# A two-layer linear-attention and MLP kernel: another order of work between the key sums and the dense layer

## The chip, the cores and the metric

The kernel runs on one core of a Trainium2 chip. Five engines work side by side there, each through its own queue of instructions in order: TensorE (PE) multiplies, VectorE (DVE), ScalarE (ACT) and GpSimd (POOL) work on rows of numbers, SyncE (SP) issues transfers. They wait for one another through semaphores. The metric is the device time of one execution in microseconds (us), as the median of several runs.

## The reference

Two identical layers, each with an attention and an MLP part, on 2048 tokens of width 576, with 32 heads of 18 and a hidden width of 4608. The weights are the same in both layers.

```python
x = x + attention(layernorm(x))
x = x + mlp(layernorm(x))          # and both lines once more

def attention(x):
    q, k, v = split_heads(x @ wqkv)                    # 32 heads of 18
    phi_q = concat(softmax(q @ w_phi), softmax(-q @ w_phi))
    phi_k = concat(softmax(k @ w_phi), softmax(-k @ w_phi))
    kv = phi_k^T @ v;  z = sum of phi_k over all tokens
    o = (phi_q @ kv) / (phi_q . z + 1e-6)
    return o @ wo

def mlp(x):
    return relu(x @ w1 + b1)**2 @ w2 + b2
```

The numbers are 32-bit floats. A product of two of them is computed as three: each operand is split into a high part in the format fp32r and a low part (the rest), and high x high, high x low and low x high are added up.

## The kernel before

**Blocks and tiles.** The tokens are worked on in four blocks of 512, each of four tiles of 128. The sums `kv` and `z` run over all tokens, so no query can be finished before the last key is in. The function `barrier` (names t0 in layer 0, t1 in layer 1) holds the passage from the one to the other, with the next stretch of work woven in so that PE has something to do. This passage is what the change edits, once in each layer.

**The passage, in order.** The queries of its block are projected, the last keys go into the sums, and the softmax parts of the queries are formed, `Q0e` to `Q3e`, one for each tile. `sums_operands` makes the operands of the attention product from the sums: `zb` (the sums of keys, spread over all partitions), and the state `kv` masked by head and split, high part `kbh` on ACT, low part `kbl` on DVE. `last_group` does this for the last group of heads, from a product with a mask, `kq`. `g_phi` then scales each tile's features by the denominator: `phi_products` forms `fm`, features times `zb`, one half on DVE and the other on POOL; `phi_sums` adds them up per head on DVE (`fu`); `phi_factors` makes the factor; `phi_scale` multiplies the features by it, half 0 on DVE and half 1 on POOL. Meanwhile PE projects the queries of another block.

`g_out` then works in two parts of two tiles each. In each part `turn` transposes the scaled features on PE (`opt`), ACT writes the high parts and DVE the low ones (`of`); `times` multiplies them with `kbh` and `kbl` (`opn`), and ACT and DVE split the result into `ooh` and `ool`, the last piece being `oolt`. Between the parts stand the scalings of tiles 2 and 3 and, for the two tiles that are done, `x_after`: 30 products with the output weights `oo0h`, `oo0l`, `oo1h`, `oo1l` (`opo`), added to the residual `ox`. After the second part the same follows for tiles 2 and 3, together with the norm of the block, `g_norm`: DVE takes statistics (`begin`) and scales the tile (`scale`), PE transposes it (`onp`; the last 64 columns of two tiles together in `transpose_rest`), ACT and DVE split it (`onh`, `onl`). Each tile then gets the bias `b2` added on POOL and is stored for the end of the MLP (`keep`).

`g_mlp` follows. `first` loads a piece of both MLP weights and splits it (high parts on ACT, low parts on POOL for the first two pieces of this block), `hidden` forms the products with the normed block (`m_3ph` in layer 0, `m_1ph` in layer 1), for the first two pieces in two halves of columns (tiles 0 and 1, then 2 and 3), `square` applies the activation, and `second` adds into the accumulators (`m_3acc`).

In layer 0 the output weights are split in this passage, high parts on ACT and low parts on POOL, and stored to memory; layer 1 loads the stored parts.

**What sets the order.** Work is given out by Python generators, and a scheduler keeps each engine's instructions in an order of its own. `tc.issue_after(ins)` puts what is issued under it behind `ins` in the queue of the engine that both use, without a wait. `held` runs a generator with each step behind named instructions, `chained` puts each step behind the step before it on DVE, ACT and POOL, and `lagged` runs a producer some steps ahead of its consumer.

Of the kernel before, what the change touches and what calls it, by code (L numbers as in the profile page):

```python
# [13 lines left out]
P = 128  # L14
# [7 lines left out]
def layers_kernel(  # L22
# [109 lines left out]
    def chained(gen, strict=False):  # L132
        ends, engines = {}, (nc.vector.engine, nc.scalar.engine, nc.gpsimd.engine)
        while True:
            traced = nc.cur_bb.bb.instructions
            mark = len(traced)
            if strict:
                ends[nc.tensor.engine] = traced_on(nc.tensor)
            with ExitStack() as behind:
                for ins in ends.values():  # L140
                    behind.enter_context(tc.issue_after(ins))
# [253 lines left out]
    def g_norm(x_of, dst, name, then=None, fine=False):  # L395
# [60 lines left out]

        if not fine:
            yield from lagged(NT, scale, turn_all)
            return
# [144 lines left out]
    def sums_operands(layer):  # L604
# [22 lines left out]
        def keep(own, parts):  # L627
            hi, lo = parts
            nc.scalar.activation(hi, own, AF.Copy)
            nc.vector.tensor_sub(lo, own, hi.bitcast(F32))  # L630


        for s in range(2):
# [12 lines left out]
        def last_group():  # L646
            w = gw[last]
            own = sb.tile([P, TB], F32, tag="hr", name=f"kq{layer}", bufs=2)
            own = own[:, : 2 * w].rearrange("p (s q f) -> p s q f", s=2, q=NQ)
            nc.vector.tensor_mul(own, kv[:, :, HG].unsqueeze(2).to_broadcast([P, 2, NQ, DH]),  # L650
                                 quarter.unsqueeze(1).unsqueeze(3).to_broadcast([P, 2, NQ, DH]))
            pt = wtile(f"kt{layer}2")
            p3 = pt[:w, : 2 * w].rearrange("p (s n) -> p s n", s=2)
            with tc.issue_after(dense["projected"].ins):
                for s in range(2):
                    nc.tensor.matmul(p3[:, s], own[:, s].rearrange("p q f -> p (q f)"),
# [77 lines left out]
    def phi_scale(e, r):  # L734
        for s in range(2):
            e3 = e[:, s].rearrange("p (h d) -> p h d", d=DH)
            (nc.gpsimd if s else nc.vector).tensor_mul(
# [30 lines left out]
    def g_out(layer, b, ph, dst, name, parts=1, pause=None, behind=None, norm=None, mid=None, costs=(None, None)):  # L768
# [50 lines left out]
        def x_after(t):  # L819
# [14 lines left out]
            return x  # L834
# [21 lines left out]
        def x_next(t):  # L856
            return xs_of[t] if t < len(xs_of) else x_after(t)

        norms = (norm or g_norm)(x_next, dst, f"{name}n", keep)
        for t in range(len(xs_of)):  # L860
            for _ in held(norms, ("part",)):
                break
        if xs_of:
# [768 lines left out]
```

## Time and profile before

| | |
|---|---|
| median of 3 runs | 2520.44 us (2519.8 to 2522.17) |
| profiled execution | 2522.92 us |
| its span (first to last instruction) | 2521.2 us |
| busy share of the span | PE 98%, PE's weight loads 86%, DVE 62%, ACT 50%, POOL 38% |
| mean granted PE clock | 0.994 |
| transfers | 348.52 MB, mean 138 GB/s |

All times in the text come from the profiled execution unless it says otherwise. An engine's busy time is the time with an instruction at work; a row that ends in a bracket gives the idle time of the engine just before the instruction and what ended it. The granted clock is the speed that PE was given, 1.00 being full.

### The profile page before, as it was taken

What the parts mean: (1) busy time and instruction counts of PE and PEld (TensorE: products, weight loads), DVE (VectorE), ACT (ScalarE), POOL (GpSimd) and SP (SyncE); (2) the same over time, 40 slices, a digit from 0 to 9 for tenths busy, and PEclk for the clock granted to TensorE, in tenths of its full rate; (3) what the DMA queues carried; (4) which work ended last, traced back from release to release, by engine and by line L of the source; (5) the groups of instructions that cost most, each with busy time, mean ns of one, the idle gap of its engine ahead of it and who ended that gap; (6) DMA issues with size and microseconds to landing.
All of it is one profiled execution on the core that took longest, in us unless ns stands there. A gap on an engine that the chain in (4) does not pass through costs nothing.

```text
span 2521.2 us, 41458 instructions
## 1 busy us (share of the span) xinstructions
PE 2477.4 (98%) x15108; PEld 2176.8 (86%) x15108; DVE 1565.9 (62%) x2514; ACT 1267.1 (50%) x2245; POOL 950.9 (38%) x1101
## 2 busy tenths in 40 slices
PE   8998999999999999999999989999999999999999
PEld 8998888888888888888889988888888888888888
DVE  6778848554856655555657778394548666555454
ACT  4344545453546666664333445454445466666642
POOL 3544312212325555552333443132123355565322
PEclk8999999999999999999999999999999999999999
DMA  9222633356434433328754144333573444333363
GB/s 333 75 70 86 203 112 88 101 167 216 130 119 119 149 109 104 117 85 283 252 185 140 44 150 131 100 98 98 163 241 100 129 129 140 118 95 114 112 199 126
DMA packets 249691, 348.52 MB, mean 138 GB/s; under 512 B 30158, under 2 KB 157262, under 8 KB 246926
## 3 DMA queue, kind: packets, MB, share of 16 engines
q1 hardware_dynamic: 248228, 343.18, 43.4%
q8 instruction: 118, 1.93, 0.3%
q10 hardware_dynamic: 1258, 2.70, 0.3%
q14 instruction: 87, 0.71, 0.1%
HBM read 279.46 MB, written 66.32 MB: 137 GB/s over the span
## 4 chain that ended last, share of the span: by engine, by line
PE 88%; DVE 4%; ACT 2%; DMA 2%; POOL 1%; issue 1%; SPq 1%; DVEq 0%; ACTq 0%; POOLq 0%
PE m_ppx L1227 8%; PE m_pacc L1256 6%; PE m_pacacc L1256 5%; PE m_1ph L912 5%; PE m_3ph L912 5%; PE m_2ph L912 5%; PE m_0ph L912 4%; PE m_ppy L1227 4%; PE m_2acc L939 3%; PE m_0acc L939 3%; PE m_1acc L939 3%; PE m_3acc L939 3%; PE m_pacacc L1246 2%; PE m_pach L1256 2%; PE m_pacc L1246 2%; PE m_ppz L1227 2%
## 5 line engine op out<-in xcount | busy, mean ns | idle before, releaser
L1217 POOL TENSOR_TENSOR m_ps<-m_pr,m_ps 128x128 fp32r<-128x128 f32 x144 | 118.8, 826 | 312.8 <-ACT m_ps L1215 251.6
L1216 DVE TENSOR_TENSOR m_ps<-m_pr,m_ps 128x448 fp32r<-128x448 f32 x144 | 96.9, 673 | 179.3 <-ACT m_ps L1215 174.4
L1256 PE MATMUL m_pacc<-m_ps,m_phb 128*128 128x448 f32 x864 | 188.5, 366 | 0.0
L1256 PEld LDWEIGHTS m_pacc<-m_ps,m_phb 128*128 128x128 f32 x864 | 162.1, 188 | 17.9
L1215 ACT ACTIVATE m_ps<-m_pr 128x576 fp32r<-128x576 f32 x144 | 98.1, 681 | 124.4 <-issue 71.6
L1256 PE MATMUL m_pacacc<-m_ps,m_phc 128*128 128x448 f32 x648 | 149.6, 368 | 0.0
L1256 PEld LDWEIGHTS m_pacacc<-m_ps,m_phc 128*128 128x128 f32 x648 | 119.8, 189 | 9.1
L1237 DVE TENSOR_TENSOR m_phb<-m_pz,m_phb 128x512 fp32r<-128x512 f32 x72 | 56.5, 784 | 111.1 <-ACT m_pz L1236 109.6
L939 PE MATMUL m_0acc<-m_0s,m_0hb 128*128 128x448 f32 x432 | 100.2, 366 | 0.0
L939 PE MATMUL m_2acc<-m_2s,m_2hb 128*128 128x448 f32 x432 | 100.1, 366 | 0.0
L912 PE MATMUL m_1ph<-t1onh,m_1h 128*128 128x512 f32 (+1 forms) x380 | 98.5, 385 | 1.5 <-DVE t1onh L443 0.8
L912 PE MATMUL m_3ph<-t0onh,m_3h 128*128 128x512 f32 (+1 forms) x380 | 98.1, 383 | 1.6 <-DVE t0onh L443 0.8
L939 PE MATMUL m_3acc<-m_3s,m_3hb 128*128 128x448 f32 x432 | 99.5, 365 | 0.0
L939 PE MATMUL m_1acc<-m_1s,m_1hb 128*128 128x448 f32 x432 | 99.5, 365 | 0.0
L912 PE MATMUL m_2ph<-a_2nh,m_2h 128*128 128x512 f32 (+1 forms) x380 | 97.9, 384 | 0.0
L912 PE MATMUL m_0ph<-a_0nh,m_0h 128*128 128x512 f32 (+1 forms) x380 | 97.8, 384 | 0.0
L939 PEld LDWEIGHTS m_0acc<-m_0s,m_0hb 128*128 128x128 f32 x432 | 80.9, 188 | 10.6 <-ACT m_0hb L920 0.2
L939 PEld LDWEIGHTS m_2acc<-m_2s,m_2hb 128*128 128x128 f32 x432 | 80.9, 188 | 10.5 <-ACT m_2hb L920 0.2
L939 PEld LDWEIGHTS m_3acc<-m_3s,m_3hb 128*128 128x128 f32 x432 | 81.0, 188 | 10.4
L939 PEld LDWEIGHTS m_1acc<-m_1s,m_1hb 128*128 128x128 f32 x432 | 81.0, 188 | 10.3
L897 POOL TENSOR_TENSOR m_1s<-m_1r,m_1s 128x128 fp32r<-128x128 f32 x36 | 25.3, 702 | 168.6 <-ACT m_1s L892 155.0
L897 POOL TENSOR_TENSOR m_3s<-m_3r,m_3s 128x128 fp32r<-128x128 f32 x36 | 24.7, 687 | 167.9 <-ACT m_3s L892 160.5
(2440 smaller groups left out, 7366.8 us busy)
## 6 DMA issues: line engine op xcount, KB each, us to landing
m_pr<-in_B_w SPq DMA_DIRECT2D x144, 288.0 KB
m_pr<-in_B_w SPq DMA_DIRECT2D x72, 256.0 KB
hd<-m_pu SPq DMA_DIRECT2D x72, 256.0 KB
m_pg<-hd SPq DMA_DIRECT2D x72, 256.0 KB
m_3r<-in_B_w SPq DMA_DIRECT2D x36, 288.0 KB
m_2r<-in_B_w SPq DMA_DIRECT2D x36, 288.0 KB
m_1r<-in_B_w SPq DMA_DIRECT2D x36, 288.0 KB
m_0r<-in_B_w SPq DMA_DIRECT2D x36, 288.0 KB
```

The costliest lines, as they stand in the source:

```text
L897: nc.gpsimd.tensor_sub(s2[:, D + R : 2 * D], r2[:, R:], s2[:, R:D].bitcast(F32))
L912: dense["hidden"] = nc.tensor.matmul(ph[:, cols], a, m, start=(k == 0), stop=(k == len(ops) - 1))
L939: nc.tensor.matmul(acc[t][:, :R], a[:, rows], m, start=(f == 0 and k == 0), stop=(f == NF - 1 and k == 2))
L1215: nc.scalar.activation(s2[:, :D], r2, AF.Copy)
L1216: nc.vector.tensor_sub(s2[:, D : D + R], r2[:, :R], s2[:, :R].bitcast(F32))
L1217: nc.gpsimd.tensor_sub(s2[:, D + R : 2 * D], r2[:, R:], s2[:, R:D].bitcast(F32))
L1227: nc.tensor.matmul(ps, a, m, start=start and i == 0, stop=i == len(ms) - 1, skip_group_check=True)
L1237: nc.vector.tensor_sub(hl, r, hh.bitcast(F32))
L1246: nc.tensor.matmul(accs[b][KC], a, m, start=(g == 0 and k == 0), stop=(g == NF - 1 and k == 2))
L1256: nc.tensor.matmul(accs[b][t][:, :R], a[:, rows], m, start=(g == 0 and k == 0), stop=(g == NF - 1 and k == 2))
```

## The change

Six edits, all between the complete key sums and the first MLP products of the block.

1. In layer 0 the split of the output weights is queued later: the high parts behind the last high part of the state (`kbh`) on ACT, the low parts behind the scaling of tile 1 on POOL. Before, both stood behind an earlier eviction.
2. The mask product `kq` moves ahead in `sums_operands` and takes another buffer.
3. The products and sums of tile 2 (`fm`, `fu`) are no longer issued ahead of the first part of `g_out`; they follow it.
4. The norm statistics of tiles 0 and 1 are taken ahead of the second part's transposes, behind DVE's scaling of tile 3.
5. After the second part, one hand-written list, `tail`, replaces the interleaving of residual products and norm: the scaling of tiles 0 and 1, all residual products of tiles 2 and 3, and only then the norm transposes. `chained` gets a mode, `every`, that orders PE's steps as well. The norm of tile 3 (`last`) goes between the hidden products of the first two weight pieces. The additions of `b2` and the stores that follow them come last.
6. The low parts of the first two pieces of MLP weights are queued behind the scaling of tile 3 on POOL.

```diff
@@ chained
+    def chained(gen, strict=False, every=False):
+        ends, engines = {}, [nc.vector.engine, nc.scalar.engine, nc.gpsimd.engine]
+        if every:
+            engines.append(nc.tensor.engine)
...
+            own = {}
             for ins in traced[mark:]:
                 if ins.engine in engines:
-                    ends[ins.engine] = ins
+                    own.setdefault(ins.engine, []).append(ins)
+            for engine, step in own.items():
+                ends[engine] = step if every else step[-1:]
@@ g_norm
+        if fine is None:
+            yield begin, scale, (transpose, split_main), (transpose_rest, split_rest)
+            return
@@ sums_operands
+        kq = sb.tile([P, KC * P], F32, tag="xn", name=f"kq{layer}")
...
+        nc.vector.tensor_mul(kq, ...)
         for s in range(2):
             pt = wtile(f"kt{layer}{s}")
...
@@ phi_scale
-            (nc.gpsimd if s else nc.vector).tensor_mul(
+            dense[f"scaled{s}"] = (nc.gpsimd if s else nc.vector).tensor_mul(
@@ g_out
         def pieces():
-            with tc.issue_after(behind.ins) if behind else nullcontext():
+            with ExitStack() as order:
+                for ins in behind or ():
+                    order.enter_context(tc.issue_after(ins.ins))
                 return wpair("o", name, low=nc.gpsimd if parts > 1 else None)
...
                 xs_of += [x_after(t) for t in range((part - 1) * NT // parts, part * NT // parts)]
+                by_part = next(g_norm(xs_of.__getitem__, dst, f"{name}n", None, None))
+                with tc.issue_after(dense["scaled0"].ins):
+                    owns = [by_part[0](t) for t in range(len(xs_of))]
...
+        def tail():
+            scaled(0)
+            yield
+            scaled(1)
+            yield
+            xs_of.append(x_after(2))
+            yield
+            owns.append(begin(2))
+            yield
+            other = g_after(3)
+            next(other)
+            yield
+            scaled(2)
+            yield
+            xs_of.append(next(other))
+            yield
+            owns.append(begin(3))
+            yield
+            pts = [main[0](t, xns[t]) for t in range(2)]
+            yield
+            for t in range(2):
+                main[1](t, pts[t])
+                yield
+            turned_rest(0)
+            yield
+            scaled(3)
+            yield
+            turned(2)
+            keep(3, xs_of[3])
+            yield
+            for t in range(3):
+                keep(t, xs_of[t])
+
+        with tc.issue_after(dense["part"].ins):
+            drain(chained(tail(), every=True))
+
+        def last():
+            turned(3)
+            yield
+            turned_rest(1)
+            yield
@@ g_mlp
-            (nc.gpsimd if early else nc.vector).tensor_sub(l1, r1, h1.bitcast(F32))
+            with tc.issue_after(dense["scaled1"].ins) if early else nullcontext():
+                (nc.gpsimd if early else nc.vector).tensor_sub(l1, r1, h1.bitcast(F32))
...
-            hidden(f, halves[0])
-        if rest:
-            with tc.issue_after(dense["hidden"].ins):
-                drain(rest)
+            with tc.issue_after(traced_on(nc.tensor)) if rest else nullcontext():
+                hidden(f, halves[0])
+                if rest:
+                    with tc.issue_after(dense["hidden"].ins):
+                        next(rest)
@@ barrier
         drain(queries)
         last_group()
-        next(phi)
         dst = {}
-        drain(g_out(layer, b, ph, dst, f"{n}o", 2, phi, dense["evicted"]))
+        drain(g_out(layer, b, ph, dst, f"{n}o", 2, phi, (kbh, scaled)))
```

Line numbers shift by 6 to 11 in the functions around `g_out`, and by 64 in the products of `g_mlp`. Below, rows of each engine's order show three places.

POOL in layer 0, from its first work behind the softmax parts of the queries on; `oo0r` and `oo1r` are the loaded output weights, `l` their low parts. Before:

```order
L336 TENSOR_TENSOR t0oo0l<-t0oo0r,t0oo0h 126x1152
L336 TENSOR_TENSOR t0oo0l<-t0oo0r,t0oo0h 72x288
L336 TENSOR_TENSOR t0oo1l<-t0oo1r,t0oo1h 126x1152
L719 TENSOR_TENSOR t0fm_2836<-t0fQ0e,zb_2802 128x576
L336 TENSOR_TENSOR t0oo1l<-t0oo1r,t0oo1h 72x288
L719 TENSOR_TENSOR t0fm_2913<-t0fQ1e,zb_2802 128x576
L737 TENSOR_TENSOR t0fQ0e<-t0fQ0e,t0fQ0r 128x576
L719 TENSOR_TENSOR t0fm_2981<-t0fQ2e,zb_2802 128x576
L737 TENSOR_TENSOR t0fQ1e<-t0fQ1e,t0fQ1r 128x576
```

The same place after:

```order
L728 TENSOR_TENSOR t0fm_2838<-t0fQ0e,zb_2802 128x576
L728 TENSOR_TENSOR t0fm_2915<-t0fQ1e,zb_2802 128x576
L746 TENSOR_TENSOR t0fQ0e<-t0fQ0e,t0fQ0r 128x576
L746 TENSOR_TENSOR t0fQ1e<-t0fQ1e,t0fQ1r 128x576
L342 TENSOR_TENSOR t0oo0l<-t0oo0r,t0oo0h 126x1152
L342 TENSOR_TENSOR t0oo0l<-t0oo0r,t0oo0h 72x288
L342 TENSOR_TENSOR t0oo1l<-t0oo1r,t0oo1h 126x1152
L342 TENSOR_TENSOR t0oo1l<-t0oo1r,t0oo1h 72x288
L728 TENSOR_TENSOR t0fm_3115<-t0fQ2e,zb_2802 128x576
```

The four low parts moved from ahead of the two tiles' products and scalings to behind them, and ahead of tile 2's product.

DVE in layer 0, from the scaling of tile 0 to the first low part of the transposed features. Before:

```order
L650 TENSOR_TENSOR kq_2973<-kv_862,quarter 128x144
L737 TENSOR_TENSOR t0fQ0e<-t0fQ0e,t0fQ0r 128x576
L731 RECIPROCAL t0fu_2916<-t0fu_2916 128x32
L719 TENSOR_TENSOR t0fm_2980<-t0fQ2e,zb_2802 128x576
L732 TENSOR_TENSOR t0fQ1r<-t0fQ1r,t0fu_2916 128x64
L725 TENSOR_REDUCE t0fu_2984<-t0fm_2980 128x32
L737 TENSOR_TENSOR t0fQ1e<-t0fQ1e,t0fQ1r 128x576
L725 TENSOR_REDUCE t0fu_2984<-t0fm_2981 128x32
L630 TENSOR_TENSOR kbl_2804<-kt_2975,kbh_2803 72x2x72
L796 TENSOR_TENSOR t0of_3016<-t0opt_3017,t0of_3016 126x256
```

After:

```order
L746 TENSOR_TENSOR t0fQ0e<-t0fQ0e,t0fQ0r 128x576
L740 RECIPROCAL t0fu_2918<-t0fu_2918 128x32
L741 TENSOR_TENSOR t0fQ1r<-t0fQ1r,t0fu_2918 128x64
L746 TENSOR_TENSOR t0fQ1e<-t0fQ1e,t0fQ1r 128x576
L639 TENSOR_TENSOR kbl_2804<-kt_2975,kbh_2803 72x2x72
L805 TENSOR_TENSOR t0of_3009<-t0opt_3010,t0of_3009 126x256
```

Tile 2's product, its two sums and the mask product no longer stand between the two scalings and the first split.

PE in layer 0, near the end of the output-weight products. Before, from the middle of the products of tile 2 into those of tile 3:

```order
L830 MATMUL t0opo_3372<-t0oo1h,t0ooh 128x288
L421 MATMUL t0onp_3344<-ident,t0onn_3326 128x128 x4
L830 MATMUL t0opo_3372<-t0oo1l,t0ooh 128x288
L830 MATMUL t0opo_3372<-t0oo1h,t0ool 128x288
L830 MATMUL t0opo_3372<-t0oo1h,t0ooh 128x288
L830 MATMUL t0opo_3372<-t0oo1l,t0ooh 128x288
L830 MATMUL t0opo_3372<-t0oo1h,t0oolt 128x288
L435 MATMUL t0onp_3409<-ident,t0one 128x128
L830 MATMUL t0opo_3416<-t0oo0h,t0ooh 128x288
L830 MATMUL t0opo_3416<-t0oo0l,t0ooh 128x288
L830 MATMUL t0opo_3416<-t0oo0h,t0ool 128x288
L421 MATMUL t0onp_3402<-ident,t0onn_3339 128x128 x4
```

After, from the last products of tile 3 on:

```order
L841 MATMUL t0opo_3406<-t0oo1l,t0ooh 128x288
L841 MATMUL t0opo_3406<-t0oo1h,t0oolt 128x288
L427 MATMUL t0onp_3431<-ident,t0onn_3334 128x128 x4
L427 MATMUL t0onp_3436<-ident,t0onn_3337 128x128 x4
L441 MATMUL t0onp_3447<-ident,t0one 128x128 x2
L427 MATMUL t0onp_3455<-ident,t0onn_3403 128x128 x4
L976 MATMUL m_3ph_3486<-t0onh,m_3h_0_3481 128x256 x5
L976 MATMUL m_3ph_3486<-t0onl,m_3h_0_3481 128x256 x4
L976 MATMUL m_3ph_3486<-t0onh,m_3h_0_3481 128x256 x5
L427 MATMUL t0onp_3501<-ident,t0onn_3452 128x128 x4
L976 MATMUL m_3ph_3519<-t0onh,m_3h_1_3514 128x256 x5
```

The norm's transposes of tiles 0 to 2 (`onp`), which stood among the products with the output weights, now stand behind the last of them, and those of tile 3 behind the first half of the first hidden products.

More of the change, by code (lines that the diff above doesn't have):

```diff
@@ L628, in keep @@
             hi, lo = parts
-            nc.scalar.activation(hi, own, AF.Copy)
+            dense["kbh"] = nc.scalar.activation(hi, own, AF.Copy)
             nc.vector.tensor_sub(lo, own, hi.bitcast(F32))
+        kq = sb.tile([P, KC * P], F32, tag="xn", name=f"kq{layer}")
+        kq = kq[:, : 2 * gw[last]].rearrange("p (s q f) -> p s q f", s=2, q=NQ)
+        nc.vector.tensor_mul(kq, kv[:, :, HG].unsqueeze(2).to_broadcast([P, 2, NQ, DH]),
+                             quarter.unsqueeze(1).unsqueeze(3).to_broadcast([P, 2, NQ, DH]))
         for s in range(2):
@@ L1400, in g_attend @@
             yield from mid[0]
-        yield from g_out(layer, b, ph, dst, name, behind=behind and behind["last"], norm=norm, mid=mid[1],
+        yield from g_out(layer, b, ph, dst, name, behind=behind and (behind["last"],), norm=norm, mid=mid[1],
                          costs=(1.0, None if norm else 3.0))
```

49 lines of the change are left out of this document (24 added, 25 removed).

## The prediction

> **What bounds the kernel now.** I read the page first, then the waits of TensorE (PE), then the chain of waits and the timelines of the two places that the change edits, the barriers t0 (layer 0) and t1 (layer 1). PE is busy for nearly the whole span, so only its idle time, or time at a low clock, can be won. The stages view cuts each barrier at four points: PE's last covered projection, the end of `t0oolt` of the first part, that of the second part, and the first product into the accumulators.
>
> ```profile
> PE 2477.4 (98%) x15108; PEld 2176.8 (86%) x15108; DVE 1565.9 (62%) x2514; ACT 1267.1 (50%) x2245; POOL 950.9 (38%) x1101
> 210.43:218.30 7.87, 1.34 (x7) 0.74 (x5) 7.87 (x15) 1.50 (x4) 4.90 (x4) 0.65 0.00 0
> 218.30:227.88 9.58, 9.58 (x62) 9.58 (x63) 6.75 (x18) 5.31 (x15) 5.07 (x5) 0.76 0.52 155
> 227.88:242.77 14.89, 13.92 (x109) 13.34 (x108) 13.52 (x33) 5.22 (x15) 2.85 (x2) 1.00 0.15 45
> 242.77:264.95 22.18, 18.31 (x134) 16.66 (x133) 13.79 (x33) 5.38 (x11) 8.79 (x12) 1.00 0.61 222
> 1456.50:1466.46 9.96, 7.96 (x69) 7.77 (x68) 8.90 (x22) 6.40 (x19) 6.95 (x6) 1.00 0.27 72
> 1466.46:1481.36 14.90, 13.93 (x109) 13.36 (x108) 13.52 (x34) 5.21 (x15) 2.85 (x2) 1.00 0.30 98
> 1481.36:1504.49 23.13, 19.35 (x134) 18.09 (x133) 13.80 (x34) 5.75 (x11) 8.80 (x12) 0.93 0.62 224
> ```
>
> In a row stand the stretch, its length, the busy time of PE, its weight loads, DVE, ACT and POOL, and the granted clock. Layer 0 needs 54.52 us from the first cut to the last, layer 1 47.99. Nearly all of the difference lies in the first part (17.45 against 9.96), though both compute the same. The chain, POOL's timeline and PE's waits say why:
>
> ```profile
> 200.52 7.78 DVE kbl L630 x2
> 1446.58 2.40 DVE kbl L630 x2
> 197.18 3.95 POOL L336 TENSOR_TENSOR t0oo0l<-t0oo0r,t0oo0h 126x1152 fp32r<-126x1152 f32 x2 [4.27 <-ACT t0oo0h L335]
> 201.10 2.67 POOL L336 TENSOR_TENSOR t0oo1l<-t0oo1r,t0oo1h 126x1152 fp32r<-126x1152 f32 x1
> 205.12 0.80 POOL L336 TENSOR_TENSOR t0oo1l<-t0oo1r,t0oo1h 72x288 fp32r<-72x288 f32 x1
> PE t0opt L793 <- DVE t0fQ1e L737: 3.4, 1, 3.4
> PE t1opt L793 <- DVE t1fQ1e L737: 2.0, 1, 2.0
> ```
>
> The same two DVE subtractions take 7.78 us beside POOL's low parts of the output weights and 2.40 us without them. DVE's chain to the scaled features Q1e is then 5.4 us late, and PE waits for it.
>
> **The change, part by part.** First part. The anchor is ACT's last sum (`zb`).
>
> ```profile
> 197.96 0.29 ACT L625 ACTIVATE zb<-z 128x144 f32<-128x144 f32 x1 [0.37 <-PE z L623]
> 1444.07 0.29 ACT L625 ACTIVATE zb<-z 128x144 f32<-128x144 f32 x1 [1.12 <-PE z L623]
> 1455.20 1.73 DVE L719 TENSOR_TENSOR t1fm<-t1fQ2e,zb 128x576 f32<-128x576 f32 x1
> 1456.99 0.73 DVE L725 TENSOR_REDUCE t1fu<-t1fm 128x32 f32<-128x576 f32 x1
> 1457.65 1.33 DVE L737 TENSOR_TENSOR t1fQ1e<-t1fQ1e,t1fQ1r 128x576 f32<-128x576 f32 x1
> 1457.18 0.73 ACT L891 ACTIVATE m_1h<-m_1r 128x640 fp32r<-128x640 f32 x1
> 1459.40 1.21 ACT L795 ACTIVATE t1of<-t1opt 126x256 fp32r<-126x256 f32 x4 [1.49 <-PE t1opt L793]
> 218.81 1.67 ACT L795 ACTIVATE t0of<-t0opt 126x256 fp32r<-126x256 f32 x4 [4.37 <-PE t0opt L793]
> ```
>
> In layer 1 the new DVE order drops the third tile's product (1455.20 to the next start at 1456.85: 1.65) and one of its sums (0.66, start to start) from before Q1e. Q1e, which ended at 1458.98, ends near 1456.65, about when PE has finished its projections. What is late next is ACT: its weight split starts at 1457.18 and ends near 1457.85, so the first eviction starts there instead of at 1459.40, 1.5 earlier. From there to `oolt` ACT and DVE pace the stage, and it moves as a whole: 9.96 becomes 8.45. The constant mask product `kq` that moves ahead lands in an idle stretch of DVE and costs nothing.
>
> Layer 0, counted from `zb`, has PE's projections end at the same point (12.47 against 12.43) but the first eviction 20.85 after it instead of layer 1's 15.33. With the low parts gone from beside DVE it follows layer 1: 8.45 instead of 17.45, **9.0 saved**. Of that, 7.0 is the eviction's earlier start, the rest the half clock in which PE comes back (0.76 over the stage). The low parts now run behind Q1e, 3.95 + 2.67 + 0.80 = 7.4 us at the most, from about 12.9 to 20.3 after `zb`; PE's first product that reads them comes near 18.0, the second weight half's from 21.2 on. That is cover of 1 to 2 us. They are SBUF work on POOL beside DVE splits that read PSUM, which in layer 1 kept their pace beside POOL's weight lows.
>
> Second part. The third tile's product and two sums, taken out above, now stand behind `oolt` and ahead of Q2e and Q3e.
>
> ```profile
> 1466.52 0.75 DVE L719 TENSOR_TENSOR t1fm<-t1fQ3e,zb 128x576 f32<-128x576 f32 x1
> 1469.17 1.69 POOL L737 TENSOR_TENSOR t1fQ2e<-t1fQ2e,t1fQ2r 128x576 f32<-128x576 f32 x1 [5.02 <-DVE t1fu L729]
> 1469.75 1.16 DVE L730 SCALAR_TENSOR_TENSOR t1fu<-t1fu 128x32 f32<-128x32 f32 x1
> 1472.26 1.64 DVE L737 TENSOR_TENSOR t1fQ3e<-t1fQ3e,t1fQ3r 128x576 f32<-128x576 f32 x1
> 1474.74 1.96 DVE L796 TENSOR_TENSOR t1of<-t1opt,t1of 126x256 fp32r<-126x256 f32 x5 [0.47 <-ACT t1of L795]
> 1481.29 1.17 DVE L389 BATCH_NORM_STATS2 t1ons<-t1ox 128x6 f32<-128x288 f32 x3
> ```
>
> That adds 0.67 + 2 x 0.66 = 2.0 to the chain to Q3e. It ended 7.45 after `oolt` and now ends 9.4 after it. PE's products of the first part cover about 6.3 of this, so PE's wait of 0.93 grows to some 2.5. Behind Q3e DVE then has the four statistics (1.17 for three, so 0.39 each) and an aggregate ahead of its first split: 1.95 in place of 0.83, so 1.1 more. The order of the remaining splits is unchanged. So 14.90 becomes **18.0 in each layer, 3.1 lost**. In layer 0 POOL's products of tiles 2 and 3 stand behind the low parts and can hold DVE's up: between 0.3 and 1.0, I take 0.5. Bounds for the loss: 2.0 if PE's head start absorbs the statistics, 4.0 if the splits also wait for ring buffers.
>
> Third stretch. Here PE's stalls go:
>
> ```profile
> 1484.16 0.66 PE L421 MATMUL t1onp<-ident,t1onn 128*128 128x128 f32 x4 [0.61 <-DVE t1onn L410]
> 1487.34 0.66 PE L421 MATMUL t1onp<-ident,t1onn 128*128 128x128 f32 x4 [1.33 <-DVE t1onn L410]
> 1499.37 0.46 PE L912 MATMUL m_1ph<-t1onh,m_1h 128*128 128x256 f32 x1 [0.82 <-DVE t1onh L443]
> 458.87 3.98 PE a_2po L830 x30
> 254.39 3.36 PE m_3ph L912 x26
> ```
>
> PE has the last 45 products of weights left at `oolt`, at 3.98 / 30 = 0.133 each: they end at T = 6.2 after it, with no norm transpose between. Scaling tile 2 now waits for tile 0's transposes, since the two share a buffer (T + 0.65); behind it in DVE's queue stand the last residual add, the statistics of tile 3 (to T + 2.4), two low parts at 0.65 and the tail's low part at 0.45: T + 4.1. PE's first hidden product that needs the tail can start there, after an idle 1.8. Its 10 remaining products (0.12 each), tile 3's transposes, 14 products, the last transposes and 28 products end at T + 11.05, and five products that stand ahead of the accumulators add 1.2: 6.2 + 12.2 = **18.4**, against 22.18 and 23.13. That saves 3.8 and 4.7. Bounds: 2.5 if the low parts slip, 6.0 if the idle 1.8 closes.
>
> Covered moves: the first two hidden weights' lows run on POOL behind Q3e and are done some 5 us before T, when PE needs them after T; the bias adds end near T + 10.5 and can hold DVE's second-layer lows by one add of 1.4, needed at T + 12.3; on SP the residual loads stand behind POOL's low-part stores, leave near 218 and are needed near 224.
>
> The sum: layer 0 8.45 + 18.5 + 18.4 = 45.35 for 54.52, so 9.2 saved; layer 1 8.45 + 18.0 + 18.4 = 44.85 for 47.99, so 3.1 saved. Together 12.3. The profiled execution took 2522.92 us (its span is 2521.2), 2.5 over the median of the runs, 2520.44; taken off the median this gives **2508.1 us**. Its own range, from the bounds, is 2503 to 2514. About 0.2% (5 us) is what a measurement here can tell from no change.
>
> **The rivals.** *The clock.* The same hidden products run at two speeds in the two layers:
>
> ```profile
> 261.13:263.77 2.64, 2.64 (x22) 2.64 (x22) 1.14 (x2) 1.15 (x2) 0.00 (x0) 1.00 1.01 423
> 1499.37:1503.53 4.16, 4.16 (x22) 4.16 (x23) 1.54 (x3) 1.74 (x3) 0.00 (x0) 0.59 1.00 413
> ```
>
> After waits as short as 0.7 and 0.8 the clock fell in layer 1 and not in layer 0, at a price of 1.5. The change makes two longer waits in each barrier (2.5 and 1.8). If each of the four costs 1.5, 6.0 of the 12.3 goes: 2514.1. Against it: the wait of 2.0 in layer 1 left the clock at 1.00 in the stretch behind it. The Trainium skill, "TensorE: Matmul & The Clock Gate", section "What's actually happening", says that the clock halves after at least one idle window of about 3.4 us; by that rule none of the four waits would cost anything, but layer 1's fall behind 0.7 and 0.8 does not agree with it, so the rival keeps its chance.
>
> *The tail gives nothing.* The waits for the norm are not removed but gathered behind the last product, where DVE's queue is one chain. If that chain takes as long as the four stalls did, the 8.5 is gone and 3.8 is left: 2516.6. For it: the chain has ten steps in a row.
>
> *It does not do what it says.* POOL's two feature products now start where the low parts stood, and if they hold `kbl` as long, 5.4 and some 2 of half clock stay: 12.3 - 7.4 = 4.9, so 2515.5. Against it: layer 1 has these products there, and its 2.40.
>
> *Slower: a load in PE's way.* Two products with the state `a_0uh` stand ahead of the accumulators in PE's order.
>
> ```profile
> 255.55 0.37 SPq L489 DMA_DIRECT2D a_0uh<-xth  x1
> 253.00:265.00 12.00, 10.08 (x74) 9.02 (x74) 6.46 (x14) 3.96 (x8) 3.61 (x4) 1.00 0.93 348
> ```
>
> Its load was issued at 255.55 and used at 263.6. Now `a_0q0l` goes ahead of it on SP. These three loads (2.7 MB) take 7.8 us at 348 GB/s; issued from T - 2, they land near T + 6 to T + 8, and PE is there at T + 11. From T + 11 on each microsecond stops PE. The kernel is slower once both layers lose over 6.2, which is a landing at T + 17; at T + 21 it loses 20 and ends at 2528. The margin of 3 us and the measured rate speak against it.
>
> **How the numbers follow.** Forecast 0.70, the clock 0.13, an empty tail 0.06, no relief 0.05, the late load 0.06. Faster by over 0.2% (under 2515.4) are the first two, 0.83; the tail and no relief lie within, 0.11; slower 0.06. The range takes the forecast's bounds and the clock's case and stops at the edge of the others: 2503.5 to 2515.5.
>
> **What would show it.** `kbl` in layer 0 near 2.4; PE's wait for Q1e gone in both layers; the stage to the first `oolt` near 8.5 in both; the second part longer, near 18, with PE's wait for Q3e near 2.5; no PE wait among the products of weights, and one of about 1.8 behind the first hidden products. It is wrong if the second part in layer 0 exceeds 20, if the third stretch stays above 21, or if PE waits for `a_0uh`.

## The result and the profile after

The changed kernel takes 2512.91 us (median of 8 runs, 2508.59 to 2515.48) against 2520.89 (8 runs, 2518.26 to 2523.24): a ratio of 0.9967, 95% interval 0.9956 to 0.9978. It is 8.0 us faster where 12.3 were forecast. The profiled span is 2513.4 us, 7.8 less than before.

The busy times on the page after, and the stages cut at the same four points as before, first layer 0, then layer 1 (stretch, length, busy time of PE, weight loads, DVE, ACT, POOL, then the granted clock):

```profile
PE 2476.7 (99%) x15108; PEld 2172.4 (86%) x15108; DVE 1558.2 (62%) x2514; ACT 1266.0 (50%) x2245; POOL 952.8 (38%) x1101
210.61:218.96 8.35, 8.24 (x69) 7.81 (x68) 5.89 (x17) 6.28 (x19) 8.35 (x7) 1.00 0.39 132
218.96:237.95 18.99, 16.93 (x113) 15.22 (x111) 16.75 (x42) 5.15 (x15) 10.14 (x11) 0.91 0.41 125
237.95:257.40 19.45, 17.16 (x130) 16.14 (x129) 13.14 (x27) 5.20 (x11) 7.15 (x8) 1.00 0.58 216
1448.26:1456.61 8.35, 8.24 (x69) 7.81 (x68) 5.89 (x17) 6.27 (x19) 3.03 (x3) 1.00 0.01 3
1456.61:1476.24 19.63, 18.05 (x113) 16.45 (x111) 16.85 (x43) 5.18 (x15) 8.20 (x10) 0.83 0.31 94
1476.24:1495.23 18.99, 17.31 (x130) 16.20 (x129) 13.44 (x28) 5.20 (x11) 7.52 (x8) 1.00 0.54 210
```

The first part is 8.35 in both layers. The second part is longer than forecast and its clock is below 1.00 in both layers, which it was in neither before. The third stretch is shorter than before, less than forecast. The sums are 46.79 (54.52 before) and 46.97 (47.99): 7.7 and 1.0 saved, 8.75 together, of which the span shows 7.8. Rows of DVE's timeline and PE's waits after (a row of waits names who waited, for whom, and how long in all, how many times, and the longest):

```profile
200.43 2.51 DVE L639 TENSOR_TENSOR kbl<-ko,kbh 126x504 fp32r<-126x504 f32 x2
226.61 1.63 DVE L746 TENSOR_TENSOR t0fQ3e<-t0fQ3e,t0fQ3r 128x576 f32<-128x576 f32 x1
PE m_3ph L976 <- DVE t0onh L449: 2.3, 1, 2.3
PE t0opt L802 <- POOL t0fQ3e L746: 1.1, 1, 1.1
PE m_1ph L976 <- DVE t1onh L449: 1.7, 1, 1.7
PE m_1acc L1003 <- DVE m_1hb L986: 0.4, 1, 0.4
PE m_1acc L1003 <- ACT m_1hb L984: 0.3, 1, 0.3
PE m_1ph L976 <- DVE m_1h L957: 0.3, 1, 0.3
```

`kbl` is back to 2.51 in layer 0, PE's waits for Q1e and for the norm among the products are gone, and three short waits of 1.0 together stand behind layer 1's third stretch, where there were none.

### The profile page after: what moved, and what is told of

It is laid out like the page before. It is cut to its first block, busy times and chain, and to the rows that moved or that the text cites. A ratio compares the mean times of both kernels' runs of the same rounds, so it can differ in the third digit from the quotient of the medians.

```text
span 2513.4 us, 41455 instructions
## 1 busy us (share of the span) xinstructions
PE 2476.7 (99%) x15108; PEld 2172.4 (86%) x15108; DVE 1558.2 (62%) x2514; ACT 1266.0 (50%) x2245; POOL 952.8 (38%) x1101
## 4 chain that ended last, share of the span: by engine, by line
PE 88%; DVE 4%; DMA 2%; ACT 2%; issue 1%; POOL 1%; SPq 1%; ACTq 0%; DVEq 0%; POOLq 0%
PE m_ppx L1292 8%; PE m_pacc L1321 6%; PE m_pacacc L1321 5%; PE m_3ph L976 5%; PE m_2ph L976 4%; PE m_0ph L976 4%; PE m_1ph L976 4%; PE m_ppy L1292 4%; PE m_2acc L1003 3%; PE m_0acc L1003 3%; PE m_3acc L1003 3%; PE m_1acc L1003 3%; PE m_pacacc L1311 2%; PE m_pacc L1311 2%; PE m_ppz L1292 2%; PE m_pach L1321 2%
## 5 line engine op out<-in xcount | busy, mean ns | idle before, releaser
L1003 PEld LDWEIGHTS m_1acc<-m_1s,m_1hb 128*128 128x128 f32 x432 | 80.9, 188 | 11.9 <-DVE m_1hb L986 0.8
L1003 PEld LDWEIGHTS m_3acc<-m_3s,m_3hb 128*128 128x128 f32 x432 | 81.1, 188 | 10.3
L1003 PEld LDWEIGHTS m_0acc<-m_0s,m_0hb 128*128 128x128 f32 x432 | 80.9, 188 | 10.5 <-ACT m_0hb L984 0.2
```

The lines of the kernel that those rows point to most:

```text
L1003: nc.tensor.matmul(acc[t][:, :R], a[:, rows], m, start=(f == 0 and k == 0), stop=(f == NF - 1 and k == 2))
```

## The experiments

Twelve kernels ran, in groups on several chips, each group with its own runs of the kernel before (medians of 2518.78 to 2520.89); the ratios compare across groups better than the medians do. The stages are cut as above, but the third stretch runs to the first product into the accumulators, 0.16 earlier than in the rows above (so 19.29 and 18.83 for the changed kernel).

| kernel | median us | ratio to before (95%) | layer 0: parts 1, 2, 3 | layer 1 |
|---|---|---|---|---|
| before | 2520.89 | | 17.5, 14.9, 22.0 | 10.0, 14.9, 23.0 |
| changed | 2512.91 | 0.9967 (0.9956 to 0.9978) | 8.3, 19.0, 19.3 | 8.3, 19.6, 18.8 |
| edit 1 alone | 2519.26 | 0.9995 (0.9986 to 1.0004) | 9.8, 21.0, 22.7 | 11.8, 14.9, 21.7 |
| edits 1 and 6 | 2513.60 | 0.9972 (0.9963 to 0.9981) | 9.8, 16.9, 22.3 | 11.9, 14.9, 21.7 |
| changed, old tail | 2515.54 | 0.9980 (0.9971 to 0.9989) | 8.3, 18.1, 22.6 | 8.3, 18.3, 21.7 |
| changed, tile 2 ahead | 2512.10 | 0.9971 (0.9962 to 0.9980) | 11.6, 16.1, 20.6 | 10.5, 16.1, 18.9 |
| changed, products twice | 2511.63 | 0.9971 (0.9959 to 0.9982) | 8.3, 17.9, 19.3 | 8.3, 17.9, 20.4 |
| changed, splits earlier | 2512.41 | 0.9971 (0.9961 to 0.9982) | 8.3, 20.0, 18.7 | 8.3, 19.3, 18.3 |
| changed, bias early | 2511.54 | 0.9970 (0.9959 to 0.9982) | 8.3, 19.9, 20.7 | 8.3, 20.3, 20.4 |
| changed, half of tile 2 ahead | 2509.65 | 0.9958 (0.9945 to 0.9970) | 8.3, 17.8, 20.9 | 8.4, 16.6, 18.8 |
| half, splits, bias | 2509.45 | 0.9965 (0.9951 to 0.9978) | 8.3, 17.8, 19.8 | 8.4, 16.7, 20.9 |
| the same with a half projection | 2512.09 | 0.9971 (0.9962 to 0.9980) | 10.1, 17.9, 20.1 | 10.3, 16.7, 21.2 |
| half and splits | 2509.26 | 0.9958 (0.9944 to 0.9971) | 8.3, 18.4, 18.7 | 8.3, 17.9, 18.3 |

**Edit 1 alone** on the kernel before (with `pieces` taking a list of instructions, as in the change):

```diff
-        drain(g_out(layer, b, ph, dst, f"{n}o", 2, phi, dense["evicted"]))
+        drain(g_out(layer, b, ph, dst, f"{n}o", 2, phi, (kbh, scaled)))
```

> The kernel before with edit 1 alone (in layer 0 the output weights' splits queued behind the state on ACT and behind tile 1's scaling on POOL). Theory A, POOL's low parts beside the state's subtraction cost layer 0 its time: the two subtractions fall from 7.78 us to about 2.5, the first part of layer 0 from 17.45 to about 10, as layer 1 has it; layer 1 stays; the total falls by 7 to 7.5 us. Rival B, the relief comes from edit 3, which takes tile 2's product and sums off VectorE's path: the subtractions stay above 6 us, the first part above 15, the total within 2 us of before.

Both were half right. `kbl` fell to 2.51 and the first part to 9.77, as A said, but nothing was won in the total. The stages of layer 0, and what DVE and POOL did at the start of the second part:

```profile
210.78:220.55 9.77, 7.94 (x69) 7.75 (x68) 8.73 (x22) 6.40 (x19) 9.24 (x6) 1.00 0.28 92
220.55:241.52 20.97, 15.90 (x109) 15.40 (x108) 18.13 (x33) 5.48 (x15) 7.36 (x7) 0.84 0.39 123
220.47 3.28 DVE L729 TENSOR_TENSOR t0fu<-t0fu,t0fQ2r 128x64 f32<-128x64 f32 x1
219.74 3.09 POOL L895 TENSOR_TENSOR m_3h<-m_3r,m_3h 128x640 fp32r<-128x640 f32 x2
222.80 0.87 POOL L899 TENSOR_TENSOR m_3s<-m_3r,m_3s 128x128 fp32r<-128x128 f32 x2
```

The output weights' low parts pushed POOL's low parts of the MLP weights back, to where DVE needs its next product: a product of 128x64 (0.21 elsewhere) took 3.28, until POOL was done at 223.67. Tile 3's product on POOL came behind them. The 7.7 won in the first part became 6.1 lost in the second. Layer 0's third stretch lost another 0.7, and layer 1, which edit 1 does not touch, lost 1.8 in its first part, where the clock fell (0.86 of full).

**Edits 1 and 6**, the same with the MLP weights' low parts behind tile 3's scaling too (one of two places in the code is shown):

```diff
-            (nc.gpsimd if early else nc.vector).tensor_sub(l1, r1, h1.bitcast(F32))
+            with tc.issue_after(dense["scaled1"].ins) if early else nullcontext():
+                (nc.gpsimd if early else nc.vector).tensor_sub(l1, r1, h1.bitcast(F32))
```

> The kernel before with edits 1 and 6: the output weights' low parts behind tile 1's scaling on POOL and the first MLP weights' low parts behind tile 3's scaling (edit 1 alone had left them ahead of tile 3's product, and VectorE's first small product of the second part took 3.28 us beside them). Theory A, what edit 1 won in layer 0's first part was given back because POOL's low parts moved beside VectorE's next work: with edit 6 the second part of layer 0 falls from 20.97 to 15 to 17, the first part stays near 9.8, and the total falls by 5 to 7 us against before. Rival B, the second part is long for another reason (the output weights' own low parts are late): it stays above 19, and the total stays within 2 us of before.

```profile
220.65:237.57 16.92, 15.42 (x109) 14.83 (x108) 14.27 (x33) 5.36 (x15) 7.80 (x7) 0.90 0.48 152
220.57 0.75 DVE L729 TENSOR_TENSOR t0fu<-t0fu,t0fQ2r 128x64 f32<-128x64 f32 x1
```

A holds: the small product takes 0.75, the second part 16.92, and the total is 0.9972 of before. The two edits of the weight splits' order alone give most of what the whole change gives: at 0.9972 (0.9963 to 0.9981) against 0.9967 (0.9956 to 0.9978), edits 2 to 5 together add nothing that is clear of the noise. On the kernel before, edit 1 needs edit 6; edit 6 alone and edit 2 alone were not tried.

**The old tail** in the changed kernel (edits 4 and 5 undone, in `g_mlp` too):

```diff
-        with tc.issue_after(dense["part"].ins):
-            drain(chained(tail(), every=True))
...
+        norms = (norm or g_norm)(x_next, dst, f"{name}n", keep)
+        for t in range(len(xs_of)):
+            for _ in held(norms, ("part",)):
+                break
```

> The changed kernel with edits 4 and 5 undone: the norm interleaved with the output products as before, its statistics behind the second part. Theory A, the new tail is worth what the stages say: the third stretch goes back from 19.29 and 18.83 to about 22 and 22 to 23, the second part loses the statistics (1.1), and the total rises by 4 to 5 us over the changed kernel. Rival B, the tail only trades short waits for long ones: the total stays within 2 us of the changed kernel.

```profile
237.95:260.54 22.59, 18.04 (x133) 16.39 (x131) 13.79 (x33) 5.79 (x11) 8.79 (x12) 1.00 0.63 217
1479.85:1501.55 21.70, 17.66 (x132) 16.20 (x131) 13.74 (x33) 5.22 (x10) 8.80 (x12) 1.00 0.60 223
```

The tail shortens the third stretch by 3.3 and 2.9 and lengthens the second by 0.9 and 1.35, a gain of 3.9 in the stages; the medians differ by 2.6 us, and the intervals of the ratios overlap. That lies between the two expectations: A has the mechanism and over-sized it.

**Products twice.** The last half of tile 1's output product is computed twice, its first result thrown away:

```diff
+                for again in range(2 if parts > 1 and t == 1 and half == 1 else 1):
                     for g in range(NG):
```

> The changed kernel with 15 products more in each barrier: the last half of tile 1's output product is computed twice, 15 x 0.133 = 2.0 us of work for TensorE where it now waits 0.36 and 1.11 us ahead of the second part's transposes. Theory A, the fallen clock of the second part costs 1 to 1.6 us in each layer: with the wait filled the clock stays at 1.00, the second part shrinks by 1.0 (layer 0) and 1.6 (layer 1), the total falls by about 2.5 us although work is added. Rival B, the chain of ScalarE and VectorE sets the pace there: the clock stays up and the second part stays within 0.3 us. Rival C, TensorE is the bound: the second part grows by up to 2 us in each layer.

```profile
219.51:237.45 17.94, 16.88 (x128) 15.82 (x126) 16.70 (x43) 5.18 (x15) 10.17 (x11) 1.00 0.43 132
1456.21:1474.15 17.94, 16.88 (x128) 15.81 (x126) 16.70 (x42) 5.18 (x15) 8.23 (x10) 1.00 0.34 103
1474.15:1494.54 20.39, 18.71 (x130) 17.60 (x129) 12.00 (x27) 5.05 (x10) 7.11 (x8) 0.92 0.60 222
```

Fifteen useless products in each barrier make the second part 1.05 and 1.69 shorter, to the same 17.94 in both layers, at a clock of 1.00: A, for the second part to the tenth. So the fallen clock cost 2.7 us in the second parts of the profiled changed kernel. In the total a median lower by 1.3 us is not clear of the noise; layer 1's third stretch lost 1.6 to a fall there.

**The changed kernel once more:**

> The changed kernel once more, to see whether its clock falls at the same places. Theory A, the pattern of short waits ahead of the second part's transposes (0.36, 1.11 and 0.2 us within 3 us, with little work between) lowers the clock each time, and the single wait of 2.3 or 1.7 us in the third stretch only at times: the second part shows 0.83 to 0.91 in both layers again. Rival B, the clock falls at random: the second part shows 1.00 in one layer or both.

```profile
218.04:237.24 19.20, 16.89 (x113) 15.30 (x111) 16.76 (x42) 5.14 (x15) 10.15 (x11) 0.91 0.41 124
1456.92:1476.18 19.26, 16.97 (x113) 15.41 (x111) 16.75 (x42) 5.14 (x15) 8.19 (x10) 0.91 0.32 96
```

Its one run took 2516.09 us. The clock fell in both layers again, and so it did in all five profiles with these waits ahead of the second part (changed, once more, old tail, splits earlier, bias early): 10 barriers of 10.

**Tile 2 ahead** (edit 3 undone):

```diff
         last_group()
+        next(phi)
         dst = {}
```

> The changed kernel with edit 3 undone (tile 2's product and sums ahead of the first part again). Theory A, the second part grew because VectorE's chain to tile 3's scaling is longer, and the wait that this makes also lets the clock fall: the second part goes from 18.99 and 19.63 to about 16 in both layers at a clock of 1.00, the first part from 8.35 to about 9.9; the total falls by 3 to 4 us. Rival B, the early statistics make the wait: the second part stays above 17.5 with a fallen clock, and the total rises by 1 us or stays.

```profile
208.46:220.04 11.58, 9.49 (x69) 9.30 (x68) 8.41 (x21) 6.40 (x19) 9.81 (x6) 0.85 0.36 116
220.04:236.13 16.09, 14.87 (x113) 13.81 (x111) 14.85 (x40) 5.18 (x15) 8.74 (x10) 1.00 0.42 133
1456.74:1472.84 16.10, 14.88 (x113) 13.83 (x111) 14.85 (x40) 5.18 (x15) 8.73 (x10) 1.00 0.27 78
```

The stages are those of A, 16.1 at full clock, but the total is that of the changed kernel: PE's wait for Q1e returns (2.1 and 2.5), and in layer 0 the clock falls there instead, and once more in the third stretch (20.6). Edit 3 as a whole is worth nothing that can be measured; it moves a wait.

**Half of tile 2 ahead.** Only DVE's half of the product and its sum stand ahead, in DVE's idle time:

```diff
+            if t == NT // 2:
...
+                with tc.issue_after(dense["scaled0"].ins):
+                    nc.vector.tensor_mul(ms[0], e[:, 0], zb[:, 0])
+                    nc.vector.tensor_reduce(u[:, 0], ...)
+                yield
+                nc.gpsimd.tensor_mul(ms[1], e[:, 1], zb[:, 1])
+                nc.vector.tensor_reduce(u[:, 1], ...)
...
+        next(phi)
         last_group()
```

> The changed kernel with half of edit 3 undone in VectorE's idle time: VectorE's half of tile 2's product and its sum (0.74 + 0.66 us) stand right behind tile 1's scaling, where VectorE idles 1.73 and 0.59 us. Theory A, the order alone counts: the first part stays at 8.35, the second falls from 18.99 and 19.63 to 16.5 to 17.5 at a clock of 1.00, the total by 3 to 4 us. Rival B, a product of VectorE that begins while POOL runs one instruction behind another waits until POOL's row ends, as the state's subtraction (7.78 us) and the small product (3.28 us) did: in layer 0 the product stands beside POOL's scaling and low parts, takes up to 7 us and adds up to 6 to the first part; in layer 1 it stands beside two products of POOL and adds 1 to 2; the total rises by 2 to 6 us.

```profile
208.54:216.86 8.32, 8.04 (x69) 7.74 (x68) 7.26 (x18) 6.28 (x19) 8.32 (x6) 1.00 0.34 113
216.86:234.66 17.80, 15.18 (x113) 13.86 (x111) 16.03 (x41) 5.18 (x15) 10.09 (x12) 1.00 0.45 143
1452.08:1468.70 16.62, 14.89 (x113) 13.86 (x111) 15.38 (x41) 5.17 (x15) 8.21 (x10) 1.00 0.32 94
207.55 1.73 DVE L758 TENSOR_TENSOR t0fm<-t0fQ2e,zb 128x576 f32<-128x576 f32 x1
206.99 1.68 POOL L746 TENSOR_TENSOR t0fQ1e<-t0fQ1e,t0fQ1r 128x576 f32<-128x576 f32 x1 [0.23 <-DVE t0fQ1r L741]
```

A holds but for layer 0's second part, 17.80 where 17.5 was the bound. DVE's product took 1.73 instead of 0.75, because POOL's scaling ran until 208.67; but it got in ahead of POOL's low parts, and DVE's idle time had room for it. The second part became 1.2 and 3.0 shorter; 1.05 and 1.69 of this are the clock, which stayed up. The median is 3.3 us under the changed kernel's, 2.3 by the ratios, whose intervals overlap; in this profile layer 0's third stretch lost 1.6 to a fall of the clock (20.9).

**Splits earlier.** In `tail`, the transposes and splits of tiles 0 and 1 stand behind `x_after(2)`:

```diff
             xs_of.append(x_after(2))
             yield
+            pts = [main[0](t, xns[t]) for t in range(2)]
+            yield
+            for t in range(2):
+                main[1](t, pts[t])
+                yield
+            turned_rest(0)
+            yield
             owns.append(begin(2))
```

> The changed kernel with another order of the tail: the norm's transposes and splits of tiles 0 and 1 stand behind tile 2's output products instead of behind tile 3's. Theory A, TensorE's wait of 2.29 and 1.68 us ahead of the first hidden products comes from VectorE's queue, in which tile 3's addition, statistics and aggregate and tile 2's scaling stand ahead of the splits: the wait goes, tile 3's own transposes wait up to 1 us instead, the third stretch falls from 19.29 and 18.83 to about 18 and 17.7, the total by 2 to 2.5 us. Rival B, the chain through tile 3's norm sets the end anyway: the wait only moves behind the first hidden products, and the third stretch stays within 0.4 us.

```profile
239.25:257.94 18.69, 17.24 (x128) 15.78 (x126) 13.71 (x27) 5.12 (x10) 7.52 (x8) 1.00 0.46 168
1475.80:1494.10 18.30, 16.73 (x127) 15.75 (x126) 13.75 (x28) 5.11 (x10) 7.54 (x8) 1.00 0.46 163
```

The wait of 2.29 and 1.68 goes; PE waits 1.0 and 1.3 for the scaled tiles 2 and 3 instead. The stretch is 0.6 and 0.5 shorter: between A and B. The total, 2512.41, is not clear of the changed kernel's.

**Bias early.** In `tail`, the additions of `b2` and their stores stand behind the scalings:

```diff
             scaled(1)
             yield
+            keep(0, xs_of[0])
+            keep(1, xs_of[1])
+            yield
             xs_of.append(x_after(2))
...
             turned(2)
-            keep(3, xs_of[3])
             yield
-            for t in range(3):
-                keep(t, xs_of[t])
+            keep(2, xs_of[2])
+            keep(3, xs_of[3])
```

> The changed kernel with the additions of b2 and their stores early: tiles 0 and 1 behind their scaling, tiles 2 and 3 behind tile 3's scaling. Theory A, the bias in last place costs 1 us behind layer 1's third stretch, since the stores stand ahead of the third MLP weight piece on SP's queue, whose load ScalarE waits 3.04 us for: without it the waits of TensorE for m_1hb (0.34 and 0.41 us) and the late load go, and the total falls by about 1 us. Rival B, POOL's additions beside VectorE's scalings and additions of the tail hold them: the third stretch grows by 1 us or more in each layer.

What ACT, POOL and SP show at this place in the changed kernel, behind layer 1's third stretch:

```profile
1487.57 5.96 POOL L870 TENSOR_TENSOR t1ox<-t1ox,b2t 128x576 f32<-128x576 f32 x4 [1.58 <-DVE t1one L417]
1489.02 4.86 SPq L871 DMA_DIRECT2D xm<-t1ox  x4
1497.08 2.10 SPq L238 DMA_DIRECT2D m_1r<-in_B_w  x2
1506.27 0.74 ACT L954 ACTIVATE m_1h<-m_1r 128x640 fp32r<-128x640 f32 x1 [3.04 <-DMA m_1r<-in_B_w]
```

The four stores wait on SP for the last additions, weight loads stand behind them, and ACT waits 3.04 for such a load. With the bias early neither ACT's wait nor any wait of PE is left in the 30 us behind the stretch. That does not show this half of A yet, for in the second profile of the changed kernel the stores stand at the same place (1488.97, 4.86), and there ACT waits 0.50 and PE not at all:

```profile
1503.65 0.74 ACT L954 ACTIVATE m_1h<-m_1r 128x640 fp32r<-128x640 f32 x1 [0.50 <-DMA m_1r<-in_B_w]
```

The total with the bias early (2511.54) is not clear of 2512.91. Its third stretches are longer by 1.4 and 1.6, as B said, but both have a clock of 0.92, and PE's wait in them is the old 2.29 and 1.67: the length is the clock's, and that the additions held the stretch is not shown.

**Half, splits and bias**, the last three diffs together:

> The changed kernel with the three edits of the runs before that helped: VectorE's half of tile 2's product and its sum behind tile 1's scaling, the transposes and splits of tiles 0 and 1 behind tile 2's output products, the additions of b2 early. Theory A, the three act in different stretches and their gains add up: first part 8.3 to 8.4, second part 17.8 (layer 0) and 16.6 (layer 1) at a clock of 1.00, third stretch 18.7 and 18.3, so 44.8 and 43.3 us, 5.3 less than the changed kernel's 46.63 and 46.81 together, and about 1 us behind them: the total falls to 2506 to 2508. Rival B, the gains share a cause (TensorE's clock, which fell in different places in each profile), and the total stays at 2509 or above.

It stays at 2509.45, as B said. With the splits earlier, the early additions do cost something, beside a fall of the clock in layer 1's third stretch (20.9). Rows of DVE and POOL:

```profile
246.65 1.61 DVE L416 TENSOR_SCALAR t0onn<-t0ox,t0onm,t0ond 128x512 f32<-128x512 f32 x1 [0.98 <-POOL t0ond L398]
246.58 1.40 POOL L881 TENSOR_TENSOR t0ox<-t0ox,b2t 128x576 f32<-128x576 f32 x1
```

DVE's scaling of tile 3 (0.55 without the early bias, in the last kernel below) is held until POOL's addition ends at 247.98, and PE waits 1.6 for it.

**A half projection** (14 products of the next block's queries) between the parts, on top of this:

```diff
-        for _ in range(4):
+        for i in range(4):
             next(phi)
-            next(queries)
-            next(queries, None)
+            for _ in range(2 if i < 3 else 0):
+                next(queries)
...
+                with tc.issue_after(traced_on(nc.tensor)):
+                    drain(fill)
```

> The kernel of the run before this with one half projection of the next block's queries (14 products, 1.95 us) moved from ahead of the first part to the place between the parts where TensorE waits 2.1 and 1.3 us for tile 3's scaling. Theory A, useful work fills the wait: the first part begins up to 1 us earlier, after VectorE's scaling of tile 1, the wait for tile 3 goes, and the clock stays up: the total falls by 2 to 3 us against the run before this. Rival B, VectorE and ScalarE set the start of the first part: TensorE waits about 1.5 us there instead, and the total stays within 1 us.

2512.09 us (ratio 0.9971, 0.9962 to 0.9980): no gain, and more likely a loss. In layer 0 the wait for tile 3 fell from 2.1 to 0.8, but PE now waited 0.4, 0.6 and 0.6 for Q1e and `kbl` in the first part and 0.9 in the second, as B said.

**Half and splits**, those two diffs without the early bias:

> The changed kernel with two of the edits tried: VectorE's half of tile 2's product behind tile 1's scaling, and the transposes and splits of tiles 0 and 1 behind tile 2's output products; the additions of b2 stay last, since in early place POOL's additions stood ahead of the statistics' power for tiles 2 and 3 and TensorE waited 1.6 and 1.9 us for the scaled tile. Theory A, without them the two edits add up: second part 17.8 and 16.6 at a clock of 1.00, third stretch 18.7 and 18.3, a sum of 45 and 43.5; the total 2506 to 2508. Rival B, the third stretch stays at 19.5 or above, since the earlier second part only moves its wait, and the total is that of the half alone, 2509.7.

2509.26 us, third stretches of 18.71 and 18.29. POOL's power was not what the additions had held: DVE waits 0.98 for it here too. The rows above show it was DVE's scaling. The two edits add up in the third stretch, but the clock fell in both second parts (0.91 and 0.90) and took 0.6 and 1.3 back. At a ratio of 0.9958 this kernel and the half alone beat the kernel before and have lower medians than the changed one by 3.3 to 3.7 us (2.3 by the ratios), but the intervals overlap.

## Why the prediction was right, and where it was too large

The first part was right in every step: 8.35 in both layers for 8.45, `kbl` at 2.51 for 2.4, no wait for Q1e; the low parts (210.69 to 217.49) were done before PE read them. Its chain in the second part was right too: Q3e ended 9.3 after `oolt` (forecast 9.4), and with the clock kept up the part is 17.94 in both layers (forecast 18.0; the 0.5 more for POOL in layer 0 did not come). PE's wait there, forecast near 2.5, came in pieces: 0.36 for Q2e, then 1.11 and 0.18 for Q3e in layer 0, with tile 2's transposes in between.

The step that was mis-sized most is the clock. The prediction had it as a rival at 0.13: four waits at 1.5, 2514.1, and the measured 2512.91 lies nearer to that than to the forecast's 2508.1. In the changed kernel it fell at two of the four, the second parts, and cost 1.05 and 1.69, not 1.5 each: 2.7 of the 3.5 that the barriers fell short. (The third stretches add 1.6; the first parts and the rest of the second came out 0.8 under their terms.) In the second profile of the same kernel the two falls cost 1.26 and 1.32. "The wait of 2.0 in layer 1 left the clock at 1.00" was the evidence against it, and one profile was too little: in the three kernels above with a wait of 1.8 to 2.5 for Q1e (edit 1 alone, edits 1 and 6, tile 2 ahead) it fell in 3 of 6 first parts. That the clock is the cause in the second parts is shown by the products computed twice. That the measured time still lies within the forecast's own bounds, 2503 to 2514, is in part luck, for none of them was drawn for the clock.

The third stretch was forecast at 18.4 and came to 19.45 and 18.99. The wait in it was put at 1.8 and measured 2.29 and 1.68; the tail's low part ended 4.15 after the last output product, forecast 4.1. In layer 1 four hidden products ran ahead of that wait, as counted; in layer 0 they ran behind it, some 0.5 later. It is so in both profiles of the changed kernel; why was not settled.

"Covered moves" missed one queue: it followed the bias additions on POOL, but not their stores on SP ahead of the weight loads. In this profile 1.0 us of waits stands behind layer 1, where the second profile has none with the same stores. So it is not shown that the stores cause these waits, and what makes 7.8 in the span of the 8.75 in the barriers stays open.

The other rivals: an empty tail is refuted by the old tail's third stretches, 3.3 and 2.9 longer, no relief by `kbl`, and no wait for `a_0uh` appeared. What the prediction took as a detail, the MLP weights' low parts behind Q3e, decides: on the kernel before, edit 1 gains nothing without edit 6.

## What to carry to other kernels

Work moved on one engine lands beside other work of a second: follow what it pushes back as well, to the next place where the two meet. A wait on TensorE has two prices, its length and a clock that may fall behind it; when both layers must wait, price a gap by both, and look at more than one profile before you call the second one nothing. A store that waits for moved work stands ahead of the loads in its queue: follow that queue too, though these runs do not show that it cost anything here.

## What the runs showed of the hardware

Two things had not been expected at this size. A VectorE instruction that begins beside one of GpSimd can be held until that one ends: 1.73 us for a product of 0.75, 1.61 for a scaling of 0.55, 3.28 for a small product of 0.21 beside four instructions in a row. Splits that read matmul results kept their pace there: two took 0.77 us beside the low parts in layer 0 (from 215.29) and 0.77 in layer 1 (from 1452.94), where POOL stood idle. The Trainium skill, "SBUF — State Buffer", section "SBUF: two separate sides", says that the two engines share a pair of ports as an exclusive lock for a whole instruction, where the VectorE instruction has two inputs in SBUF or runs in a two-port mode. These durations agree with it; why VectorE passed between two of GpSimd's instructions near 208.7 in one kernel and not near 221.3 in another is left open.

The clock fell to 0.50 in 10 of 10 barriers that had the short waits for Q2e and Q3e (0.36, 1.11 and mostly 0.2 us, with five transposes between the first two): six times for 3.4 us, four times for 6.8. After a single wait it fell only at times: behind 1.3 or 2.1 us in 2 of the 6 second parts of the three kernels with half of tile 2 ahead and nothing moved between the parts, behind 1.8 to 2.5 in 3 of the 6 first parts named above, and behind 2.29 or 1.68 in 5 of the 12 third stretches with that wait.

The times at which the traces record a change of the clock say when. In all 14 traces every change from 60 us on stands on one beat of 3.413 us. The rows give nine such beats (PE's busy time behind the length, the clock third from the end). The first two show the changed kernel's fall in layer 0, the next two its wait of 2.29 there, the next three its fall in layer 1, and the last two the wait of 2.29 in the kernel with tile 2 ahead:

```profile
226.37:229.78 3.41, 1.70 (x9) 0.84 (x9) 3.41 (x8) 1.12 (x4) 3.32 (x3) 1.00 0.02 5
229.78:233.20 3.42, 3.42 (x15) 3.06 (x16) 2.76 (x10) 1.30 (x5) 3.25 (x7) 0.50 0.41 112
243.44:246.85 3.41, 2.68 (x22) 2.22 (x20) 1.95 (x6) 1.90 (x4) 0.01 (x1) 1.00 0.92 343
246.85:250.27 3.42, 1.86 (x15) 1.86 (x16) 2.97 (x6) 0.00 (x0) 1.75 (x3) 1.00 1.03 419
1462.00:1465.41 3.41, 1.96 (x15) 1.49 (x14) 3.41 (x6) 0.00 (x0) 1.95 (x3) 1.00 0.34 128
1465.41:1468.82 3.41, 3.28 (x12) 2.36 (x13) 3.41 (x12) 1.21 (x4) 3.41 (x3) 0.50 0.05 15
1468.82:1472.23 3.41, 3.41 (x18) 3.39 (x18) 2.01 (x7) 1.85 (x6) 2.33 (x6) 0.50 0.61 177
242.76:246.18 3.42, 1.54 (x13) 1.08 (x11) 3.07 (x8) 1.89 (x4) 0.77 (x2) 1.00 1.02 416
246.18:249.59 3.41, 3.00 (x14) 3.00 (x15) 1.85 (x4) 0.00 (x0) 2.14 (x2) 0.50 0.75 314
```

In the changed kernel the wait of 2.29 is shared by two beats and the clock stays up; with tile 2 ahead it lies in one, and the next runs at half. Over all traces, from 60 us on to 8 us before the end, each of the 33 falls stands behind a full-clock beat in which PE was busy for 0.7 to 2.2 us. All 17 beats with at most 1.55 us were followed by a fall, 16 of the 68 with 1.59 to 2.17, and none of some 9900 with more. So where a wait lies on the beat counts beside its length, and one profile does not settle whether a wait lowers the clock. The Trainium skill, "TensorE: Matmul & The Clock Gate", section "What's actually happening", puts the fall behind at least one idle window of about 3.4 us, in windows that run freely. The beat agrees with these windows; the idleness does not, since PE was busy for up to 2.2 us of the beat ahead of a fall.
